# Threshold attention and a feed-forward block on one core: weight chunks begun at other points of slots six to nine, and the first loads in another order

## The chip, the core and the metric

The kernel runs on one core of a Trainium2 chip. A core has five engines that run at the same time and wait for one another by semaphores: TensorE (PE, matrix products; its weight loads are listed as PEld), VectorE (DVE), ScalarE (ACT), GpSimd (POOL) and SyncE (SP), which in this kernel only issues transfers. Each engine executes its own instructions in the order in which the program gives them. The metric is the device time of one execution in microseconds (us).

## The reference

Attention over 8 batches, 8 heads, 576 positions and head size 64, in which a score counts only if it lies within tau of the largest of its row; then a feed-forward block with a layer norm and a residual.

```python
scores = scale * np.matmul(q, k.transpose(0, 1, 3, 2))
thresh = np.max(scores, axis=-1, keepdims=True) - tau
scores = np.where(scores >= thresh, scores, -1000000000.0)
scores = scores - np.max(scores, axis=-1, keepdims=True)
attn = np.exp(scores)
attn = attn / (np.sum(attn, axis=-1, keepdims=True) + 1e-09)
x = np.matmul(attn, v)            # then (B,H,S,D) -> (B, S, H*D), 512 features
xn = (x - mean(x)) / np.sqrt(var(x) + 1e-06) * g_ln
out = x + np.maximum(xn @ w_ch1, 0.0) @ w_ch2    # 512 -> 2048 -> 512
```

q, k, v and out are 32-bit floats. The two weight matrices arrive as 64-bit floats, and the kernel turns them into 32-bit floats on the chip while attention is already running.

## The kernel before, in words

**Slots.** The work is cut into 72 slots, nine for each batch. A unit is one batch and one pair of heads. Slots 0 to 3 of a batch take the first 256 queries of the four units, slot 4 takes the 64 queries that are left over in all four, and slots 5 to 8 take the second 256 queries. One slot is a chain: `scores` (line 400) makes the scores on PE; `exponentials` (line 423) takes the row maxima on DVE (line 431), the thresholds on POOL (line 435) and the exponentials on ACT (line 445); `weights` (line 447) compares the scores with the thresholds, multiplies and sums, all in one DVE instruction of line 452 for each of four blocks. From slot 6 on POOL divides the four blocks (line 468), DVE transposes them in 32 by 32 blocks (`turn_blocks`, line 542), SP sends the result to device memory and fetches it back in another layout (lines 549 to 574), and PE multiplies with v in the following slot (`values_of`, line 611). In slots 0 to 5 PE transposes instead, by products with diagonal matrices.

**Loading.** `load_qk` fetches q and k of a unit in eight transfers, `load_v` fetches v in four (three from batch 1 on). `turn` (line 352) scales q on POOL (line 364) and transposes k and q on DVE (lines 368 to 381); `turn(u)` stands in the slot before the one that needs unit u. The q and k tiles of the units have one buffer each, so that a unit can only be loaded when the unit before it has been transposed. The first unit alone lies in the room of the tile xc, which is needed only later (`qk_room`, line 152).

**Feed-forward.** A group is half a batch, 288 tokens, and there are 16. The first layer of a group is 64 products of PE (line 801 to 806), the second layer of the first group another 64 (`second_plain`, line 835). Four parts of a slot, called quarters, each issue a share of these products (`second_part`, line 1016), so that the first group is spread over the 18 quarters from the start of slot 6. The order of PE's products is thus written out in advance; `ended` (line 321) only keeps a product from being written into the order ahead of the conversion of its weights. Two PSUM banks take the results of the products in turn, and ACT empties them (lines 809 and 848).

**Conversion of the weights.** Class `Weights` (line 178) handles 32 chunks of 128 by 512 numbers: 0 to 15 are w_ch1, 16 to 31 are w_ch2. A chunk is fetched raw (512 KB, `fetch`) into room that is free at that time, each with a note up to which chunk it may stay there. Then it takes four steps: `begin` is two DVE instructions (lines 274 and 278) that build the 32-bit number from the high word, and it queues two ACT passes over the raw words (lines 284 and 287); `carry` is an integer add on POOL (line 299) that needs both; `mask` is a DVE instruction (line 305) that needs the carry and frees the raw room; `scale` (POOL, line 315) multiplies w_ch1 by g_ln. The table `BEGUN` says for each slot up to which chunk is begun at three points: behind the row maxima and `turn`, ahead of `weights` (first number); behind `weights`, beside POOL's divisions (second); and at the end of the slot, behind the transposes of `turn_blocks` (third). `mask_all` stands ahead of the first two points and, from slot 6 on, behind `turn_blocks` (line 1164).

**Order of a slot on each engine**, as the loop from line 1085 writes it: scores; maxima; first quarter of products; `turn`; masks and begins; second quarter; carries and scales; `weights` with its divisions; masks and begins; third quarter; carries; block transposes and transfers; masks; product with v of the slot before; fourth quarter; begins; carries.

Of the kernel before, what the change touches and what calls it, by code (L numbers as in the profile page):

```python
# [12 lines left out]
ALU = mybir.AluOpType  # L13
# [5 lines left out]
def kernel(  # L19
# [31 lines left out]
    nc = tc.nc  # L51
# [4 lines left out]
    HP = H // 2  # L56
# [3 lines left out]
    NB = S // 32  # L60
# [18 lines left out]
    scl_sb = consts.tile([128, 1], F32, name="scl_sb")  # L79
# [13 lines left out]
    units = [(b, hp) for b in range(B) for hp in range(HP)]  # L93
    loaded, values_in, turned = {}, {}, {}
# [32 lines left out]
    def load_v(u):  # L127
        b, hp = units[u]
        vt = ins.tile([128, 2, J, D], F32, tag="v", name="v_in")
        vr = v_rest[hp]  # L130
        both = v[b, 2 * hp : 2 * hp + 2]
        if b:
            nc.sync.dma_start(
                out=vt.rearrange("p h c d -> p h (c d)"),
                in_=both[:, : J * 128].rearrange("h (p c) d -> p h (c d)", c=J),
            )
        for h in range(0 if b else 2):
            nc.sync.dma_start(
                out=vt[:, h], in_=both[h, : J * 128].rearrange("(c p) d -> p c d", p=128)
            )  # L140
        for j in range(2):
            nc.sync.dma_start(
                out=vr[64 * j : 64 * j + 64, j], in_=both[:, J * 128 :].rearrange("h p d -> p h d")
            )
        values_in[u] = (vt, vr)
# [8 lines left out]
    load_qk(1, (nc.sync, nc.scalar))  # L154
    for t in v_rest:
        nc.gpsimd.memset(t, 0.0)
    load_v(0)
    nc.scalar.preload_act_table_set("natural_log_exp_and_others")
    make_identity(nc, ident)
    nc.vector.memset(eps_sb, 1e-6)  # L160
# [17 lines left out]
    class Weights:  # L178
# [88 lines left out]

        def begin(self):
            i = self.begun
            assert all(self.raw[j][0] > i or self.raw[j][0] == 10 for j in range(self.masked, i))  # L270
            self.begun += 1
            hi = self.words(i, U32)[:, :, 1]
            au = self.chunks[i][0].bitcast(U32)
            nc.vector.tensor_scalar(
                out=au, in0=hi, scalar1=3, scalar2=0x3FFFFFFF,
                op0=ALU.logical_shift_left, op1=ALU.bitwise_and,
            )
            nc.vector.scalar_tensor_tensor(  # L278
                out=au, in0=hi, scalar=0xC0000000, in1=au,
                op0=ALU.bitwise_and, op1=ALU.bitwise_or,  # L280
            )
            low, low_in, top = self.words(i, I32), self.words(i, U32), self.words(i, F32)[:, :, 1]
            self.on_scalar += [
                lambda: nc.scalar.activation(
                    low[:, :, 0], low_in[:, :, 0], func=AF.Copy, scale=2.0**-29
                ),
                lambda: nc.scalar.activation(top, top, func=AF.Square),
            ]
# [59 lines left out]
    def by_blocks(n):  # L348

        return n >= FIRST  # L350

    def turn(u):

        q_in, k_in = loaded.pop(u)
        qT = att.tile([128, 2, QH], F32, tag="qT", bufs=4, name="qT")  # L360
        kT = att.tile([128, S], F32, tag="kT", bufs=4, name="kT")
        ql = q_last[u % HP]
        for at in (slice(0, 8), slice(8, NB)) if u == 0 else (slice(0, NB),):
            nc.gpsimd.tensor_scalar(
                out=q_in[:, at], in0=q_in[:, at], scalar1=scl_sb, scalar2=1.0,
                op0=ALU.mult, op1=ALU.mult,
            )
        nc.vector.transpose(kT, k_in.rearrange("p n c -> p (n c)"))
        for s in range(2):
            part = q_in[:, 9 * s : 9 * s + 8]  # L370
            if by_blocks(units[u][0] * SLOTS + units[u][1] + (HP + 1 if s else 0)):
                nc.vector.transpose(
                    qT[:, s].rearrange("p (j a c) -> p a j c", j=2, a=4),
                    part.rearrange("p (a j) c -> p a j c", j=2),
                )
            else:
                nc.vector.transpose(qT[:, s], part.rearrange("p n c -> p (n c)"))
        nc.vector.transpose(
            ql.rearrange("p (t c) -> p t c", t=2),
            q_in.rearrange("p (t n) c -> p t n c", t=2)[:, :, 8],  # L380
        )
        turned[u] = (qT, kT, ql)
# [672 lines left out]

    conversion = Weights()
    if w_ch1.dtype == I64:
        conversion.fetch(3)
    else:
        for i in range(NK):  # L1060
            nc.sync.dma_start(out=w1_sb[i], in_=w_ch1[i * 128 : (i + 1) * 128])
            nc.scalar.mul(w1_sb[i], w1_sb[i], g_sb[:, i : i + 1])
        for i in range(ND):
            nc.sync.dma_start(
                out=w2_sb[:, :, i],
                in_=w_ch2[i * 128 : (i + 1) * 128, :].rearrange("p (m c) -> p m c", m=NK),
            )
        conversion.begun = conversion.carried = len(conversion.chunks)
        conversion.masked = conversion.fetched = conversion.begun
        conversion.scaled = conversion.n1  # L1070

    BEGUN = [
        (0, 0, 2), (3, 3, 4), (5, 5, 6), (7, 7, 8), (9, 9, 10), (11, 11, 12),
        (14, 17, 19), (21, 22, 24), (26, 27, 28), (30, 31, 32), (32, 32, 32),
    ]

    def constants(times):
# [4 lines left out]

    constants(14)
    turn(0)
    for n in range(NS):
        b, s = divmod(n, SLOTS)
        masks_at, behind_at, end_at = BEGUN[min(n, len(BEGUN) - 1)]
        run(n, -3)
        if 0 < n <= HP:
            constants(8 if n > 1 else 26)  # L1090
        scores(b, s)
        run(n, -2)
        run(n, -1)
        if n == FIRST + 1:
            conversion.take(e_room[1])
        rest = exponentials(n)
        es, thr = next(rest)
        run(n, 0)
        if n == HP + 2:
            next(rest, None)  # L1100
        if n >= HP:
            conversion.fetch(3)
        run_first(stores)
        second_part(n, 0)
        while drops and drops[0][0] is nc.gpsimd:
            drops.pop(0)[-1]()
        next(rest, None)

        u = (n + 1) // SLOTS * HP + (n + 1) % SLOTS
        if (n + 1) % SLOTS < HP and u < len(units):  # L1110
            turn(u)
            if u + 1 < len(units):
                load_qk(u + 1)
        if n < HP:
            conversion.fetch(2)
        if n < SLOTS + HP:
            run_all(aside)
        conversion.mask_all()
        conversion.begin_to(masks_at)
        if n <= HP + 1:  # L1120
            conversion.carry_all()
            conversion.scale_all()
        run(n, 1)
        second_part(n, 1)
        conversion.carry_all()
        conversion.scale_all()
        blocks_go = by_blocks(n)
        diags = weights(es, thr, blocks_go)
        run_all(aside)
        drip()  # L1130
        if n < SLOTS:
            run_all(stores)
        conversion.mask_all()
        conversion.begin_to(behind_at)
        run(n, 2)
        second_part(n, 2)
        conversion.carry_all()
        box = []
        if blocks_go:
            conversion.fetch(3, wait=0)  # L1140
            scr = turn_blocks(b, s, es)
            at_quarter(n + 1, 0, lambda b=b, s=s, scr=scr, box=box: box.append(fetch(b, s, scr)))
        else:

            made = turn_weights(s, es, diags)
            for i, at in enumerate(
                (-1, -1, 0, 0)
            ):
                if i < 3:
                    at_quarter(n + 1, at, next, made)  # L1150
                else:
                    at_quarter(n + 1, at, lambda made=made, box=box: box.append(next(made)))
        at_quarter(
            n + 1, 1 if b == 0 and s <= HP else 3,
            lambda b=b, s=s, box=box: values_of(b, s, box[0]),
        )
        if s in (HP, 2 * HP):
            group_ready(2 * b + (s > HP))
        run_all(aside)
        drip({nc.vector: 4, nc.gpsimd: 6})  # L1160
        if HP <= n < FIRST:
            conversion.fetch(3)
        if n >= HP + 2:
            conversion.mask_all()
        run(n, 3)
        if b == 0 and s < HP - 1:
            load_v(s + 1)
        elif n >= SLOTS - 2 and (n + 2) % SLOTS < HP and n < NS - 2:
            load_v((n + 2) // SLOTS * HP + (n + 2) % SLOTS)
        second_part(n, 3)  # L1170
        conversion.begin_to(end_at)
        conversion.carry_all()
        run_all(aside)
        drip({nc.vector: 2, nc.gpsimd: 0})
# [40 lines left out]
```

## Time and profile before

| what | value |
|---|---|
| time, median of 3 runs | 1355.61 us (1354.12 to 1357.16) |
| time of the profiled execution | 1354.76 us |
| span of its trace | 1352.6 us |
| PE busy | 1317.1 us (97%) |
| DVE busy | 883.2 us (65%) |
| POOL busy | 630.1 us (47%) |
| ACT busy | 459.1 us (34%) |
| start of the scores of slots 6, 7, 8, 9, 10, 11 | 74.96, 100.95, 126.03, 147.40, 168.79, 187.97 us |

The profile is a page and a trace of one execution. The page has the busy time of each engine, forty slices of the span with the busy share of each in tenths, the chain of work that ended last, and groups of instructions with the mean time of one. The trace can be asked for one stretch: what each engine did in order of time, who waited for whom, and how busy each engine was. A wait is put down to whatever came last by the records. The start of a slot is read from PE's instructions of line 417. The profiled execution took 2.2 us more than its span.

### The profile page before, as it was taken

How to read it: one execution, taken by the hardware profiler on the slowest of the kernel's cores; microseconds unless marked ns; L12 is line 12 of the kernel's file. 1: busy time of each engine (PE TensorE's matmuls, PEld its weight loads, DVE VectorE, ACT ScalarE, POOL GpSimd, SP SyncE). 2: the span in 40 equal slices, each digit the busy share in tenths (PEclk: the TensorE clock that was granted, in tenths of full speed). 3: DMA queues.
4: the chain of work that ended last, by engine and by line, in shares of the span. 5: the costliest groups of instructions: out<-in, count | busy, mean ns of one | idle time of the engine just before them, and what ended most of it. 6: DMA issues, size and time to landing. Idle time of an engine off the chain costs nothing.

```text
span 1352.6 us, 40467 instructions
## 1 busy us (share of the span) xinstructions
PE 1317.1 (97%) x17400; PEld 993.9 (73%) x17400; DVE 883.2 (65%) x1544; ACT 459.1 (34%) x995; POOL 630.1 (47%) x836
## 2 busy tenths in 40 slices
PE   8997999999999999999999999999999999999997
PEld 6764557869687786968778696876869677686957
DVE  6989987667755675666766667556756667666112
ACT  4875432332423323232333323233232323323120
POOL 3567665445444444444534554444444445335313
PEclk9998999999999999999999999999999999999999
DMA  9816874457644775437744576446764376343211
GB/s 171 257 60 186 218 207 150 177 159 183 189 139 146 194 193 172 151 131 190 194 146 155 138 203 179 151 146 186 191 178 151 120 194 187 124 159 129 85 18 20
DMA packets 335300, 213.94 MB, mean 158 GB/s; under 512 B 247377, under 2 KB 292689, under 8 KB 327057
## 3 DMA queue, kind: packets, MB, share of 16 engines
q1 hardware_dynamic: 329008, 210.46, 54.2%
q8 instruction: 137, 2.24, 0.7%
q10 hardware_dynamic: 5952, 0.74, 0.4%
q0 software_dynamic: 160, 0.15, 0.1%
q14 instruction: 43, 0.34, 0.1%
HBM read 124.00 MB, written 87.29 MB: 156 GB/s over the span
## 4 chain that ended last, share of the span: by engine, by line
PE 88%; DVE 5%; DMA 2%; ACT 2%; SPq 2%; issue 1%; POOL 1%; POOLq 0%; ACTq 0%; DVEq 0%
PE p L101 36%; PE seg L101 30%; PE sc L417 10%; PE sc L611 8%; PE sc L621 2%; DVE e L452 1%; DVE w L278 1%; SPq L118 1%; PE tp L101 1%; DVE w L305 1%; ACT e L445 1%; DMA k_in<-in_k_dram 1%; DVE et L542 1%; PE var L101 1%; DVE neg L431 0%
## 5 line engine op out<-in xcount | busy, mean ns | idle before, releaser
L101 PE MATMUL p<-xc,w 128*64 128x288 f32 x4096 | 519.0, 409 | 12.1 <-ACT hidden L809 6.5
L101 PEld LDWEIGHTS p<-xc,w 128*64 128x64 f32 x4096 | 288.8, 137 | 220.0 <-issue 16.2
L431 DVE TENSOR_REDUCE neg<-sc 128x2 f32<-128x1152 f32 x144 | 188.7, 1352 | 278.1 <-PE sc L417 278.1
L468 POOL TENSOR_SCALAR e<-e,den 128x576 f32<-128x576 f32 x264 | 207.8, 799 | 135.9 <-DVE den L457 135.9
L101 PE MATMUL seg<-hidden,w 128*64 128x144 f32 x3840 | 247.9, 287 | 0.0
L101 PEld LDWEIGHTS seg<-hidden,w 128*64 128x64 f32 x3840 | 234.9, 137 | 11.5 <-issue 8.5
L452 DVE SCALAR_TENSOR_TENSOR e<-sc,thr,e 128x576 f32<-128x576 f32 x288 | 222.4, 811 | 17.9 <-POOL thr L435 11.2
L435 POOL TENSOR_SCALAR thr<-neg,low_sb 128x2 f32<-128x2 f32 x144 | 41.6, 289 | 378.0 <-DVE neg L431 377.4
L809 ACT ACTIVATE hidden<-p 128x288 f32<-128x288 f32 x256 | 106.1, 416 | 296.4 <-PE p L101 296.4
L445 ACT ACTIVATE e<-sc,neg 128x576 f32<-128x576 f32 x288 | 197.4, 753 | 2.5 <-DVE neg L431 2.5
L542 DVE STREAM_TRANSPOSE et<-e 128x1152 f32<-128x1152 f32 x118 | 161.2, 1373 | 14.3 <-POOL e L468 13.8
L417 PE MATMUL sc<-kT,qT 64*64 64x384 f32 (+3 forms) x2048 | 139.4, 403 | 3.5 <-DVE e L452 3.1
L611 PE MATMUL sc<-em,v_in 128*64 128x128 f32 (+1 forms) x2368 | 129.9, 263 | 2.9 <-DVE w L305 2.3
L611 PEld LDWEIGHTS sc<-em,v_in 128*64 128x64 f32 x2368 | 122.8, 137 | 11.5 <-DVE o L723 2.5
L101 PE MATMUL seg<-hidden,stage 128*64 128x144 f32 x1920 | 123.3, 286 | 0.0
L101 PEld LDWEIGHTS seg<-hidden,stage 128*64 128x64 f32 x1920 | 117.6, 137 | 2.9 <-issue 2.9
L634 ACT COPY x<-sc 128x128 f32<-128x128 f32 x120 | 31.6, 265 | 236.2 <-PE sc L417 171.0
L882 POOL TENSOR_TENSOR hidden<-hidden 128x576 f32<-128x576 f32 x60 | 84.8, 1428 | 51.9 <-ACT hidden L809 42.3
L417 PEld LDWEIGHTS sc<-kT,qT 64*64 64x64 f32 x2048 | 76.1, 133 | 44.5 <-issue 20.9
L897 ACT COPY part<-seg 128x288 f32<-128x288 f32 x74 | 29.8, 403 | 190.6 <-PE seg L101 190.1
L882 DVE TENSOR_TENSOR hidden<-hidden 128x576 f32<-128x576 f32 x60 | 51.2, 888 | 51.5 <-PE seg L101 48.5
L818 POOL TENSOR_TENSOR hidden<-hidden 128x288 f32<-128x288 f32 x48 | 38.9, 810 | 54.6 <-ACT hidden L816 52.1
(131 smaller groups left out, 1093.7 us busy)
## 6 DMA issues: line engine op xcount, KB each, us to landing
scr<-et SPq DMA_DIRECT2D x63, 1152.0 KB, 5.0
em<-scr SPq DMA_DIRECT2D x63, 1024.0 KB, 5.8
q_in<-in_q_dram SPq DMA_DIRECT2D x124, 72.0 KB, 2.7
out_dram<-ot SPq DMA_DIRECT2D x248, 36.0 KB, 3.8
k_in<-in_k_dram SPq DMA_DIRECT2D x120, 72.0 KB, 3.0
er<-scr SPq DMA_DIRECT2D x132, 64.0 KB, 5.2
v_in<-in_v_dram SPq DMA_DIRECT2D x28, 256.0 KB, 5.5
w<-in_moe_w_ch_dram SPq DMA_DIRECT2D x11, 512.0 KB, 6.4
```

Source lines behind the costliest of these rows:

```text
L101: nc.tensor.matmul(out[r], lhsT=lhsT[:, r], rhs=rhs, **flags)
L417: nc.tensor.matmul(sc[h][64 * i : 64 * i + 64, at : at + n], lhsT=ql[r] if s == HP else qT[r, half, j * 128 + 64 * i : j * 128 + 64 * i + 64],
L431: nc.vector.tensor_reduce(out=neg[:, i], in_=pairs[h], axis=AXL.X, op=ALU.max, negate=True,)
L435: nc.gpsimd.tensor_scalar(out=thr[:, i], in0=neg[:, i], scalar1=-1.0, scalar2=low_sb, op0=ALU.mult, op1=ALU.add,)
L445: nc.scalar.activation(es[:, i], blocks[i], func=AF.Exp, bias=neg[:, i : i + 1])
L452: nc.vector.scalar_tensor_tensor(out=es[:, i], in0=blocks[i], scalar=thr[:, i : i + 1], in1=es[:, i], op0=ALU.is_ge, op1=ALU.mult, accum_o ...
L468: nc.gpsimd.tensor_scalar(out=es[:, i], in0=es[:, i], scalar1=den[:, i : i + 1], scalar2=1.0, op0=ALU.mult, op1=ALU.mult,)
L542: nc.vector.transpose(et[:, :, 64 * h : 64 * h + 64].rearrange("p n (j c) -> p j n c", j=2), es[:, 2 * h : 2 * h + 2].rearrange("p j (n c) ...
L611: nc.tensor.matmul(dst[64 * h : 64 * h + 64], lhsT=vt[:, h, c, :], rhs=pick(em[:, 2 * j : 2 * j + 2, c], h), start=c == 0 and first, stop= ...
L809: nc.scalar.activation(hidden[:, d], p1, func=AF.Relu)
L818: nc.gpsimd.tensor_tensor(out=sq[:, 0], in0=sq[:, 0], in1=sq[:, c], op=ALU.add)
L882: eng.tensor_tensor(out=out[at], in0=in0[at], in1=in1[at], op=op)
```

## The change

Three things are altered.

The loads at the start. The first two raw chunks are fetched ahead of everything but the first two units. The third unit's q and k go into the first unit's room (`qk_room`), as soon as that unit has been transposed; v of the first unit and two more chunks follow. The fourth unit is loaded where the third was, one slot earlier than it was before, and the fifth again where it was.

Scaling q. For units 1 to 3 POOL's scaling is taken out of `turn` and stands ahead of the row maxima of the slot (`scale_q`).

The conversion. In slots 6 to 9 the table has two or three chunks at the first point, three (in slot 9 two) at the second and none at the end of a slot. The masks behind `turn_blocks` are gone, so that chunks begun at the second point are masked in the next slot, behind its maxima. The check in `begin` on how long a raw chunk may lie in the room of a later one is widened by six chunks.

```diff
-    load_v(0)
     nc.scalar.preload_act_table_set("natural_log_exp_and_others")
...
-            assert all(self.raw[j][0] > i or self.raw[j][0] == 10 for j in range(self.masked, i))
+            assert all(self.raw[j][0] + 6 > i or self.raw[j][0] == 10 for j in range(self.masked, i))
...
+    def scale_q(u, q_in):
+
         for at in (slice(0, 8), slice(8, NB)) if u == 0 else (slice(0, NB),):
             nc.gpsimd.tensor_scalar(
                 out=q_in[:, at], in0=q_in[:, at], scalar1=scl_sb, scalar2=1.0,
                 op0=ALU.mult, op1=ALU.mult,
             )
+
+    def turn(u):
...
+        if not 0 < u < HP:
+            scale_q(u, q_in)
...
     if w_ch1.dtype == I64:
-        conversion.fetch(3)
+        conversion.fetch(2)
...
         (0, 0, 2), (3, 3, 4), (5, 5, 6), (7, 7, 8), (9, 9, 10), (11, 11, 12),
-        (14, 17, 19), (21, 22, 24), (26, 27, 28), (30, 31, 32), (32, 32, 32),
+        (15, 18, 18), (20, 23, 23), (25, 28, 28), (30, 32, 32),
...
     turn(0)
+    load_qk(2, room=qk_room.rearrange("p c t -> p (c t)"))
+    load_v(0)
+    conversion.fetch(2)
     for n in range(NS):
...
+        if n + 1 < HP:
+            scale_q(n + 1, loaded[n + 1][0])
         rest = exponentials(n)
...
             turn(u)
-            if u + 1 < len(units):
-                load_qk(u + 1)
+            if u + 1 < len(units) and u != 2:
+                load_qk(u + 1 if u > 1 else 3)
         if n < HP:
-            conversion.fetch(2)
+            conversion.fetch(2 if n else 1)
...
         if HP <= n < FIRST:
             conversion.fetch(3)
-        if n >= HP + 2:
-            conversion.mask_all()
         run(n, 3)
```

More of the change, by code (lines that the diff above doesn't have):

```diff
@@ L350, in by_blocks @@
         return n >= FIRST
[L352 to L362, printed above, removed]
+    def scale_q(u, q_in):
         for at in (slice(0, 8), slice(8, NB)) if u == 0 else (slice(0, NB),):
@@ L367, in turn @@
             )
+    def turn(u):
+        q_in, k_in = loaded.pop(u)
+        if not 0 < u < HP:
+            scale_q(u, q_in)
+        qT = att.tile([128, 2, QH], F32, tag="qT", bufs=4, name="qT")
+        kT = att.tile([128, S], F32, tag="kT", bufs=4, name="kT")
+        ql = q_last[u % HP]
         nc.vector.transpose(kT, k_in.rearrange("p n c -> p (n c)"))
```

## The prediction

> **What bounds the kernel now.** I read the page first. PE is busy 97% of the span, so most of the run can only be moved by PE's idle time. The busy slices show where that lies: the first ninth.
>
> ```profile
> PE 1317.1 (97%) x17400; PEld 993.9 (73%) x17400; DVE 883.2 (65%) x1544; ACT 459.1 (34%) x995; POOL 630.1 (47%) x836
> ...
> DVE  6989987667755675666766667556756667666112
> ```
>
> Then engine time per stretch, one stretch from scores to scores for each of slots 6 to 10 (columns: us, and busy time of PE, PEld, DVE, ACT, POOL).
>
> ```profile
> 74.96:100.95 25.99, 25.04 (x273) 16.44 (x277) 20.28 (x34) 17.32 (x34) 17.72 (x23) 1.00 0.01 2
> 100.95:126.03 25.08, 18.54 (x181) 10.81 (x176) 24.77 (x35) 12.07 (x25) 19.33 (x18) 0.86 0.71 199
> 126.03:147.40 21.37, 18.72 (x196) 11.21 (x192) 20.68 (x34) 10.67 (x21) 12.13 (x14) 1.00 0.77 172
> 147.40:168.79 21.39, 18.73 (x196) 11.48 (x192) 20.73 (x35) 9.18 (x18) 14.32 (x15) 1.00 0.89 233
> 168.79:187.97 19.18, 17.54 (x189) 10.59 (x184) 16.62 (x32) 6.31 (x13) 11.12 (x15) 1.00 0.78 202
> ```
>
> In slots 7 to 9 DVE is the full engine (24.77 of 25.08), PE idles 2.6 to 6.5 us a slot. In slot 6 DVE has a gap. From slot 11 on PE is full, so what slots 0 to 10 win or lose is passed on unchanged to the end. The waits, of DVE (8 to 200 us) and of PE (80 to 190 us), name the gaps (us in total, times, longest):
>
> ```profile
> DVE w L305 <- POOL w L299: 5.3, 1, 5.3
> ...
> DVE kT L368 <- DMA k_in<-in_k_dram: 1.8, 1, 1.8
> DVE qT L377 <- POOL q_in L364: 0.9, 2, 0.4
> ```
>
> ```profile
> PE p L101 <- ACT hidden L809: 9.0, 2, 6.5
> PE sc L611 <- DVE w L305: 2.3, 1, 2.3
> PE p L101 <- DVE w L305: 1.6, 1, 1.6
> ```
>
> The 1.8 and 0.9 us are the opening: slots 1, and 0 and 2. The 5.3 us are slot 6, first mask against first carry. PE's 1.6 us are at 178.04, in slot 10: the products of the last chunk (31) wait for its mask (177.33, line 305). That wait ends the stage.
>
> The timeline (start, duration) gives the price of a begin, here two in slot 8:
>
> ```profile
> 137.09 0.42 DVE L274 TENSOR_SCALAR w<-e 128x512 uint32<-128x512 uint32 x1
> 137.54 0.69 DVE L278 SCALAR_TENSOR_TENSOR w<-e,w 128x512 uint32<-128x512 uint32 x1
> 138.15 0.42 DVE L274 TENSOR_SCALAR w<-x_room 128x512 uint32<-128x512 uint32 x1
> 138.61 1.72 DVE L278 SCALAR_TENSOR_TENSOR w<-x_room,w 128x512 uint32<-128x512 uint32 x1
> ```
>
> The first takes 137.09 to 138.15, 1.06 us. The second takes 2.10, because POOL began the first one's carry at 138.47 (1.31 us). Beside divisions (slot 6, 97.01 to 99.83, two begins) one takes 1.41. A mask alone takes 0.60.
>
> [...] 0.69 us becomes 1.72, about the rest of the carry. [...] SP stood at the transfer of line 549 for 34.4 us from slot 5 to 6.
>
> **The change, part by part.** All sums are against the profiled execution, 1354.76 us (span 1352.6 plus 2.2 around it), 0.85 under the median; I add the same difference to the median, 1355.61.
>
> *Opening.* Unit 2's eight transfers were issued at 15.24 to 22.36, behind 1.5 MB of chunks (issued 11.34 to 13.92), and k landed at 24.6, when DVE had been free since 22.95. Now SP issues two chunks (about 8.4 to 9.4, behind unit 1's q, which ended at 8.35), unit 2 (its room is free at 9.15; eight at 0.5 to 0.6 us: to about 15), four of v, two chunks, unit 3, one chunk. Estimated from those rows, k of unit 2 lands near 19, before it is needed at 22.5: the 1.79 us go. So do the 0.45 us in slot 0: POOL scales q ahead of the thresholds, under PE's scores and the maxima; in slot 0 the scaling waits for unit 1's q (8.35 plus some 4 us of landing, 12.3), and the thresholds queued behind it on POOL are wanted by `weights` only at 14.65. In slot 2 the 0.44 us also go from DVE, but PE's warm-up products run from 40.76 right up to the scores at 42.60, so there PE becomes last and nothing is won. Chunk 2, begun at about 25.2, is issued near 17.5 and lands some 5.5 us later (the median at that time): covered by 2 us. v of unit 0 is wanted at 24.8 and lands near 21. Sum: -2.2. Two-sided bound: -2.7 if PE gives way, +1 if a chunk in front delays unit 1's k (needed at 13.06).
>
> *Slots 6 to 9 on DVE.* All 21 begins (12 to 32) and masks remain; only their neighbours change. I walk each slot with the prices above, up to the maxima of the next.
> Slot 6: one begin more ahead of the masked scores falls into the 5.3 us wait, free. The first carry still ends at 92.8 (POOL's sums of squares at 88.95 to 91.52 hold it). Three masks follow carries at 1.27 us each: to about 97.1. Three begins beside divisions (4.2): 101.3. Transposes (2.55): 103.9, against 108.92 before, where three masks (3.45) and two begins (3.1) followed. -5.0.
> Slot 7: one mask more beside scales (+0.8). After `weights` come the root of the variance (2.7) and two masks, by which time the divisions are done; of the three begins the second and third meet the carries of the one before: 2 x 2.1 = +4.2. Gone: a mask and two begins behind the transposes (0.57 + 1.06 + 2.06). +1.3.
> Slot 8: one mask more (+0.6). Only two of four divisions outlast `weights` (143.76 to 146.30), and two masks and one begin use them up (143.59 to 146.76): again two begins beside carries, +4.2. Gone: mask and begin at 149.65 to 151.91, -2.3. They had covered POOL's residual add at 149.80; now the output transpose waits for it, +1.0. +3.5.
> Slot 9: two masks more (+1.2), begin 31 beside a carry (+2.1), gone mask and begin 170.21 to 171.84 (-1.6). +1.7.
> Sum: -5.0 + 1.3 + 3.5 + 1.7 = +1.5 at slot 10's maxima. The title's "beside divisions only" holds in slot 6 alone. Two-sided bound on the five begins beside carries (7, 8, 9): 5 x 1.04 = 5.2 us less if ACT's passes (line 284), and so the carries, come too late to meet them; 2 us more if the first begins of the rows collide too.
>
> *What PE waits for then.* Mask 30 was behind slot 9's transposes; now it stands where mask 31 stood. Eight products of PE need chunk 30 or 31, not four, and the mean of group 1 lies between. After the wait PE has 8 x 0.485 + 0.48 = 4.36 us to the first product of group 1, against 4 x 0.485 = 1.94. +2.4. DVE's scaling of x (line 686) and slot 10's transposes come later behind it; the product that uses them was at 200.99 and em's fetch at 191.59, some 5 us of cover.
> Waits earlier on PE (chunk 15's scale in slot 7, mask 25 in slot 9) grow by 1 to 3 us each, but PE reaches the scores some 3 us before DVE: nothing.
>
> *SP.* Chunk 31 is now fetched in slot 9 behind em and er of slot 8, not in slot 8. er ended at 161.5 before; the issue comes near 163, and with 6.4 us (the median landing) the chunk is there at 169.4. DVE wants it at 168.5; that wait lies beside the carry which would have held it anyway: nothing.
>
> Sum: -2.2 + 1.5 + 2.4 = +1.7: 1356.5 in the profiled execution, **1357.3** against the median.
>
> **Rivals.**
> *Faster: the carries miss the begins.* At 92.8 POOL was late because ACT was held by PE's results; were that so in slots 7 to 9, five begins cost 1.06. 1357.3 - 5.2 = 1352.1. Against it: in slot 8 the carry followed each begin within 0.25 us.
> *Begins do lie beside divisions*, as the title says: 5 x 0.69 less, 1353.9.
> *Slower: the opening's wait moves on.* Place: unit 1's k (ACT's queue) or chunk 2, with 1 MB of chunks now ahead. Nothing is won once DVE gets k of unit 2 or chunk 2 1.8 to 2.2 us late, that is k after 24.7 or chunk 2 after 27.4. 1357.3 + 2.2 = 1359.5. For it: DMA is 90% busy from 9 us on. Against: big packets moved 340 to 416 GB/s at 15 to 18 us.
> *Slower: chunk 31.* Slow landings of 9.4 us (slot 5's) would put it at 172.4, 2.3 us behind the cover of the carry at 170.1; with masks 25 to 27 late too, about 1360.5. It decides above a landing of 7 us.
>
> **How the numbers follow.** About 0.2% (2.7 us) is what a measurement of this kernel can tell from no change: faster is below 1352.9, slower above 1358.3. Chances: main sum 0.45 (own range 1355 to 1360; 0.27 same, 0.18 slower); carries miss 0.17 (0.14 faster, 0.03 same); begins beside divisions 0.06 (0.05 same, 0.01 faster); opening lost 0.20 (0.04 same, 0.16 slower); chunk 31 0.12 (0.02 same, 0.10 slower). Together faster 0.15, same 0.41, slower 0.44. Range: 1352.2, the faster rival, to 1361, past the slower ones.
>
> **What the profile after would show.** Opening right: no wait of DVE on k_in, scores of slot 3 (42.60) at about 40.4. Slot 7's maxima near 101.7 (108.92 less 5.0 and 2.2). Line 278 at over 1.6 us seven or eight times in slots 6 to 9, not four (107.3, 129.8, 138.6, 158.9). PE waiting for line 305 in slot 10 four products earlier, for several us. I am wrong if slot 10's mask 30 comes earlier than mask 31 did less 2.2 us (175.1), or if SP's queue holds chunk 31.

## The result, and the profile after

The changed kernel takes 1358.84 us (median of 9 runs, 1357.59 to 1360.26), the kernel before, run alongside, 1354.66 (9 runs, 1353.91 to 1357.16): a ratio of 1.0029, interval 1.0019 to 1.0039. It is 4.2 us slower; I had forecast 1.7 us slower. The profiled execution took 1360.19 us with a span of 1358.1, 5.5 us more than that of before. It is one of the slowest of the nine, 1.35 us above their median, so the two profiles lie further apart than the medians do. One execution of the variants below, of pe_kept_busy, ran at a mean granted clock of 0.56 from end to end (2300 us) and counts in no ratio.

In the changed kernel the mask is line 304, the carry 298, a begin 273 and 277, the maxima 435 and the scores 421; L101 is the helper that records most products. The page, busy time and DVE's slices:

```profile
PE 1320.2 (97%) x17400; PEld 993.8 (73%) x17400; DVE 885.2 (65%) x1544; ACT 459.3 (34%) x995; POOL 630.0 (46%) x836
...
DVE  7989967766755675666766667556756667666112
```

No engine has more instructions to run. DVE is busy 2.0 us longer and PE, with the same 17400 matmuls, 3.1 us longer. That last number is the odd one: equal work should take equal time. The stretches from scores to scores of slots 6 to 10 show where (us, then busy time of PE, PEld, DVE, ACT, POOL; then PE's granted clock):

```profile
73.94:101.22 27.28, 25.48 (x272) 16.25 (x276) 22.59 (x37) 17.89 (x34) 19.00 (x24) 1.00 0.01 2
101.22:119.65 18.43, 16.85 (x181) 10.13 (x177) 17.95 (x29) 9.39 (x22) 15.64 (x15) 1.00 0.78 210
119.65:147.49 27.84, 20.84 (x197) 12.63 (x192) 27.08 (x38) 13.99 (x26) 16.31 (x16) 0.94 0.74 179
147.49:167.80 20.31, 18.50 (x196) 11.52 (x192) 18.74 (x34) 7.59 (x14) 11.51 (x14) 1.00 0.89 232
167.80:193.14 25.34, 20.12 (x188) 11.61 (x184) 18.69 (x32) 6.67 (x14) 12.30 (x16) 0.87 0.69 181
```

Up to slot 10's scores nothing is lost (167.80 against 168.79). Slot 10 then takes 25.34 us where it took 19.18, and slot 11's scores stand at 193.14 against 187.97: +5.17, and the distance stays between 5.2 and 5.8 to the end. In this row PE is busy 20.12 us with 188 matmuls; before it was 17.54 with 189. Its clock column reads 0.87.

The waits of DVE (8 to 200 us), then of PE (80 to 195 us):

```profile
DVE neg L435 <- PE sc L421: 6.0, 3, 4.6
DVE w L304 <- POOL w L298: 4.3, 1, 4.3
DVE xc L690 <- PE mean L101: 3.6, 1, 3.6
...
DVE w L273 <- DMA hidden<-in_moe_w_ch_dram: 1.4, 1, 1.4
```

```profile
PE p L101 <- DVE w L304: 5.2, 1, 5.2
...
PE p L101 <- ACT hidden L813: 5.0, 5, 2.5
```

Three things are new. PE waits 5.2 us for a mask, where it waited 1.6. DVE in turn waits 3.6 us for the mean from PE, and 4.6 us for scores in slot 11, both behind that one wait. And the opening's wait for k of unit 2 is gone, but one of 1.4 us for chunk 2 has come. Group 1 is the second group of tokens; its first products are the ones from xc. The timeline of PE in slot 10 (start, duration; four matmuls of the records are one product):

```profile
169.85 3.13 PE L101 MATMUL p<-hidden,w 128*64 128x288 f32 x24
178.21 3.15 PE L101 MATMUL p<-hidden,w 128*64 128x288 f32 x12 [5.22 <-DVE w L304]
181.14 1.17 PE L101 MATMUL mean<-sum,avg_sb 128*64 128x288 f32 x4
182.10 3.27 PE L101 MATMUL p<-hidden,w 128*64 128x288 f32 x20
185.21 4.53 PE L101 MATMUL p<-xc,w 128*64 128x288 f32 x36
```

The same place in the kernel before:

```profile
178.04 2.16 PE L101 MATMUL p<-hidden,w 128*64 128x288 f32 x16 [1.65 <-DVE w L305]
180.03 4.54 PE L101 MATMUL p<-xc,w 128*64 128x288 f32 x36
```

Ahead of the wait 24 matmuls take 3.13 us, behind it 12 of the same take 3.15. From the end of the wait to the first product of group 1 it is 7.00 us (1.99 before), not the 4.36 that I had counted. The changed kernel's stretch in windows, columns as above:

```profile
172.98:178.20 5.22, 0.01 (x1) 0.00 (x0) 4.77 (x9) 2.80 (x5) 2.59 (x5) 0.85 0.89 265
178.20:179.80 1.60, 1.59 (x8) 0.86 (x10) 0.56 (x1) 0.00 (x0) 0.00 (x0) 0.50 0.70 221
...
183.00:185.20 2.20, 2.20 (x18) 1.22 (x16) 2.20 (x6) 0.00 (x0) 0.00 (x0) 0.89 0.65 105
```

The granted clock falls to a half during the wait, some 3.7 us into it, and comes back only near 183.4, after 5.2 us of products: half of those, 2.6 us, are lost. The kernel before has the same, in a place where it cost nothing: slot 7's wait of 6.5 us, windows of PE around it:

```profile
105.65:112.19 6.54, 0.01 (x1) 0.01 (x1) 6.47 (x8) 3.94 (x9) 4.41 (x6) 0.79 0.88 222
112.19:116.20 4.01, 4.01 (x18) 2.07 (x20) 3.94 (x7) 2.48 (x5) 3.18 (x3) 0.50 1.01 259
```

18 matmuls in 4.01 us; DVE, busy for 3.94 of them, hid it. The number that told of it, 0.86 in the clock column of slot 7, stands in the view that the prediction shows first.

The products behind the waits of 5.22 and 6.54 us ran at a granted clock of 0.50. Behind slot 10's wait of 1.65 us in the kernel before it was 1.00 (178.04 to 182), and behind one of 2.62 us it was 0.52 (old_begins_two_masks, below); the last section puts the waits side by side.

So the new theory, the **clock theory**: slot 10's loss is the wait for mask 30, the 4 products and the mean that it now holds up (+2.4, as forecast), and 2.6 us of half clock, which the wait itself brings about.

### The profile page after: what moved, and what is told of

It is laid out like the page before. It is cut to its first block, busy times and chain, and to the rows that moved or that the text cites. A ratio compares the mean times of both kernels' runs of the same rounds, so it can differ in the third digit from the quotient of the medians.

```text
span 1358.1 us, 40472 instructions
## 1 busy us (share of the span) xinstructions
PE 1320.2 (97%) x17400; PEld 993.8 (73%) x17400; DVE 885.2 (65%) x1544; ACT 459.3 (34%) x995; POOL 630.0 (46%) x836
## 4 chain that ended last, share of the span: by engine, by line
PE 87%; DVE 3%; DMA 3%; SPq 3%; ACT 2%; issue 1%; POOL 0%; POOLq 0%; DVEq 0%; ACTq 0%
PE p L101 34%; PE seg L101 30%; PE sc L421 10%; PE sc L615 8%; PE sc L625 2%; DVE e L456 1%; ACT e L449 1%; DMA em<-scr 1%; PE tp L101 1%; SPq L118 1%; DMA k_in<-in_k_dram 1%; DVE et L546 1%; PE mean L101 1%; SPq L553 1%; PE var L101 0%
## 5 line engine op out<-in xcount | busy, mean ns | idle before, releaser
L101 PE MATMUL p<-xc,w 128*64 128x288 f32 x4096 | 517.8, 408 | 7.7 <-ACT part L901 4.6
L101 PEld LDWEIGHTS p<-xc,w 128*64 128x64 f32 x4096 | 286.9, 137 | 216.4 <-issue 14.3
L101 PE MATMUL seg<-hidden,w 128*64 128x144 f32 x3840 | 247.9, 287 | 0.0
L101 PEld LDWEIGHTS seg<-hidden,w 128*64 128x64 f32 x3840 | 234.9, 137 | 11.5 <-issue 8.5
L101 PE MATMUL seg<-hidden,stage 128*64 128x144 f32 x1920 | 123.3, 286 | 0.0
L101 PEld LDWEIGHTS seg<-hidden,stage 128*64 128x64 f32 x1920 | 117.6, 137 | 2.9 <-issue 2.9
```

The lines of the kernel that those rows point to most:

```text
L101: nc.tensor.matmul(out[r], lhsT=lhsT[:, r], rhs=rhs, **flags)
```

## Experiments

All are variants of the changed kernel except where said. Times are medians; ratios are to the kernel before, run alongside (medians 1354.62 to 1354.92 us). A ratio is not the quotient of the two medians and differs from it by up to 0.0007, 1 us; where two variants were not run side by side, their intervals say more than the difference of their medians.

**PE kept busy.** Constants go through PE where it would idle, with no use made of the products:

```diff
         conversion.begin_to(masks_at)
+        if n == SLOTS + 1:
+            constants(20)
```

> The changed kernel, with 20 products of constants (into a free bank, results unused) put on PE between the 24 products before mask 30 of slot 10 and those that wait for it. At 0.23 us each (as in the opening) they fill 4.6 of the 5.2 us of idling and end before the mask (178.16). Clock theory: of the 5.2 us lost, 2.64 are the products after the wait at half the granted clock (7.00 us from mask 30 to the first product of group 1, against 4.36 counted); PE kept busy keeps the clock at 1.00, and the time falls by 2.6, from 1358.8 to 1356.2. Rival, the place theory: the products are slow there for another reason (transfers of 300 to 400 GB/s at 178 to 183 us, operands just written), and the time stays at 1358.8 with the 7.0 us unchanged.

> The same kernel as pe_kept_busy (20 products of constants ahead of the wait for mask 30), for its profile, since the profiled execution of the first was at about half the clock from end to end. Clock theory: PE's clock column reads 1.00 from 173 to 185 us, and from mask 30's end to the first product of group 1 it takes about 4.4 us (7.05 in the changed kernel). If half clock is only part of it, more than 5 us at clock 1.00.

Measured: 1356.97 us, ratio 1.0013 (1.0007 to 1.0020), so 1.9 us below the changed kernel's median (the two intervals just touch), where 2.6 had been expected; the single run of the second gave 1356.26. PE's timeline in the second:

```profile
171.65 4.54 PE L101 MATMUL warm<-ident,avg_sb 128*64 128x128 f32 x80
...
177.52 1.68 PE L101 MATMUL p<-hidden,w 128*64 128x288 f32 x12 [0.86 <-DVE w L304]
...
181.94 4.54 PE L101 MATMUL p<-xc,w 128*64 128x288 f32 x36
```

From the wait's end to group 1 it is now 4.42 us, with the clock at 1.00 in every window from 172.9 to 186; 12 matmuls take 1.68. DVE's part and the mask's place are as in the changed kernel. The transfers are there too (283 and 304 GB/s at 177.6 to 182), so the place theory falls: 4.42 is the 4.36 that I had worked out, and the other 2.6 us are the clock, in these two profiles. The medians show 1.9 of the 2.6; why not all is not shown. Adding work to PE made the kernel faster.

**The parts alone.** First the opening alone, from the changed kernel. The third call of the masks is the call of `mask_all` behind `turn_blocks`, which the change had taken out:

```diff
-        (15, 18, 18), (20, 23, 23), (25, 28, 28), (30, 32, 32),
+        (14, 17, 19), (21, 22, 24), (26, 27, 28), (30, 31, 32), (32, 32, 32),
...
             conversion.fetch(3)
+        if n >= HP + 2:
+            conversion.mask_all()
         run(n, 3)
```

> The changed kernel with the old table of begins and the third call of the masks back: only the opening's part of the change is left. Opening theory: it gains 1.0 us (as slot 3's scores, 42.61 to 41.61, show in the changed kernel), not the 2.2 that I forecast, since chunk 2 lands late: 1353.7 against 1354.7, slot 10's mask 31 at about 176.3. Rival: the forecast's 2.2 would have come without the new begins, then 1352.5. Second rival: slot 6 or SP's queue takes the 1.0 back, then 1354.7.

Measured: 1354.00 us, ratio 0.9989 (0.9980 to 0.9997): 0.8 us won, near the first value (the interval, -2.7 to -0.4 us, holds the rival's 2.2 as well). Its profiled execution is no guide to the opening, since half clock fell on slot 2's scores there (28 matmuls in 3.85 us, 2.16 elsewhere; granted clock 0.55 from 31.2 to 35).

Then the conversion alone: the kernel before, with the new table, without the third call of the masks, and with the wider assertion.

```diff
-        (14, 17, 19), (21, 22, 24), (26, 27, 28), (30, 31, 32), (32, 32, 32),
+        (15, 18, 18), (20, 23, 23), (25, 28, 28), (30, 32, 32),
...
-        if n >= HP + 2:
-            conversion.mask_all()
```

> The kernel before with the new table of begins, the third call of the masks gone, and the wider assertion: only the conversion's part of the change. Clock theory: DVE's mask 30 comes 1.2 us later than mask 31 did (+1.2), 4 products more and the mean after it (+2.4), half clock after the idling (+2.6): +6.2, 1360.9. If the two parts are not additive, because the later opening lets PE's idling stay short of what brings the clock down, +3.6: 1358.3.

Measured: 1359.32 us, ratio 1.0040 (1.0028 to 1.0053): 4.5 us lost, between the two values. The parts add up: -0.8 + 4.5 = +3.7, against +4.2 for both. In its profile PE idles only 3.49 us for mask 30 and the clock falls all the same, just after PE has resumed (1.00 in the wait, 0.63 in the first 0.80 us behind it, then 0.50); from there to group 1 it is 6.11 us, 1.7 more than at full clock.

**Chunk 2 first**, the other term that was off. In the changed kernel SP's timeline reads:

```profile
10.01 4.30 SPq L118 DMA_DIRECT2D qk_room<-in_q_dram  x4
14.36 4.09 SPq L118 DMA_DIRECT2D qk_room<-in_k_dram  x4
...
22.45 1.07 SPq L257 DMA_DIRECT2D hidden<-in_moe_w_ch_dram  x2
```

Unit 2's eight transfers hold SP for 8.4 us, and chunk 2 is issued at 22.45 and landed 3.9 us later, 1.4 us after DVE wanted it.

```diff
-        conversion.fetch(2)
+        conversion.fetch(3)
...
     load_v(0)
-    conversion.fetch(2)
+    conversion.fetch(1)
```

> The changed kernel with chunk 2 fetched together with chunks 0 and 1, ahead of unit 2's q and k (one chunk in place of two behind v). Opening theory: DVE's wait for chunk 2 (1.4 us) goes; k of unit 2 comes about 1 us later, near 20, still before 22.1; PE's warm-up then ends last in slots 2 and 3 (28.65 against scores at 29.07), so 0.4 to 1.0 us is won: 1358.8 becomes 1357.8 to 1358.4. If nothing but DVE bound the opening, the whole 1.4: 1357.4.

Measured: 1358.80 us, ratio 1.0029 (1.0019 to 1.0038): nothing, a miss. The wait for chunk 2 is gone, DVE does not wait for k, and slot 3's scores come at 40.35, where the prediction had put them (40.4; the changed kernel 41.60). Slot 10's scores are 1.6 us earlier (166.21) and slot 11's 1.2 (191.90), PE's wait for mask 30 being 5.56 us. The profiled execution is 1.3 us shorter than the changed kernel's, but that one lay 1.35 above its own median and this one lies on it: the pair of profiles overstates the gain, and what the medians lose again is not shown. With the masks mended (below) the same edit gives medians lower by 0.8 and 1.45 us, but the intervals of the ratios overlap almost wholly, so a gain of this edit is not shown there either.

**Mask 30 ahead of the maxima.** The third call of the masks in slot 9 alone:

```diff
+        if n == SLOTS:
+            conversion.mask_all()
         run(n, 3)
```

> The changed kernel with the third call of the masks back in slot 9 alone, so that masks 30 and 31 stand behind slot 9's transposes, ahead of slot 10's maxima (about 172 to 173.3). Clock theory with the place of mask 30 as the whole cause: PE does not idle there, the clock stays at 1.00, the first product of group 1 then waits for DVE's scaling of x at about 179.2 instead of 185.2: 6 us less than the changed kernel, 1352.8 to 1353.9. Rival: the begins in slots 7 to 9 are what costs, and the masks' place only shows it: then the wait moves on to the next thing that DVE delivers, and less than 3 us come back, 1356 or more.

Measured: 1354.20 us, ratio 0.9991 (0.9983 to 0.9999), 4.6 us below the changed kernel. PE's timeline in slot 10:

```profile
171.09 4.59 PE L101 MATMUL p<-hidden,w 128*64 128x288 f32 x36
...
179.88 4.59 PE L101 MATMUL p<-xc,w 128*64 128x288 f32 x36 [0.55 <-ACT o L852]
```

Masks 30 and 31 stand at 172.1 and 172.7, PE waits for neither, and group 1 starts at 179.88 instead of 185.21. The place of mask 30 is the cause of the loss. The time is 0.3 to 1.4 us more than expected. Ahead of group 1 PE waits 0.52 us for POOL's sum and 0.55 for ACT, and the clock falls once more, in slot 9 after two short waits (0.78 and 1.62 us):

```profile
160.60:163.50 2.90, 0.51 (x8) 0.28 (x6) 2.83 (x10) 0.59 (x2) 2.37 (x4) 1.00 1.01 274
163.50:167.60 4.10, 4.10 (x37) 3.38 (x39) 4.03 (x7) 0.90 (x2) 4.10 (x4) 0.60 0.79 155
```

That fall is not what kept the rest back: both_mended (below) keeps the clock at 1.00 there, and from DVE's first instruction of `weights` in slot 9 to group 1 it takes 20.12 us as against 20.11 here. What did is open.

**Table or masks.** The remaining two of the four combinations. In the first only the old table is put back, in the second only the third call of the masks, from slot 6 on.

> The changed kernel with the old table of begins, and the third call of the masks still gone: it tells the table from the masks. Masks theory (what costs is that mask 30 comes behind slot 10's maxima, whichever table): masks 30 and 31 both stand there, mask 30 at about 175.7 to 176.4, PE idles some 3.4 us for it and has 4.4 us to go to group 1 (7 if the clock falls): 0.7 to 3.3 us behind the kernel before, 1355.3 to 1357.9. Table theory (what costs is the begins' place): like opening_alone, 1354.0.

> The changed kernel with the third call of the masks back in every slot from slot 6 on, and the new table of begins. Masks theory: only the one in slot 9 counts, so it is like third_mask_slot9: 1353.7 to 1354.7. Table theory: the new begins still cost DVE 1.4 us in slots 6 to 9, and it stands that much behind opening_alone: 1355.4.

| median, us (ratio's interval) | third call gone | third call from slot 6 on | in slot 9 alone |
|---|---|---|---|
| old table | 1355.66 (0.9999 to 1.0015) | 1354.00 (0.9980 to 0.9997) | - |
| new table | 1358.84 (1.0019 to 1.0039) | 1355.96 (0.9999 to 1.0015) | 1354.20 (0.9983 to 0.9999) |

Without the third call the old table loses too, 1.7 us against the same table with it: mask 30 comes behind the maxima, at 175.16, PE idles 2.62 us, the clock falls right after (0.52 from 175.86 to 179.40), and it takes 6.1 us to group 1. That is the masks theory's value. The new table with all three calls is a miss for it: 1355.96, not 1353.7 to 1354.7, and nearer to the table theory's 1355.4. In that profile three masks stand between the transposes and the next maxima in slots 6 and 7: slot 7's maxima come at 105.76 (103.38 in the changed kernel), slot 8's at 129.55 (126.16), slot 10's at 175.05 (172.59). So the third call is needed in slot 9 whichever the table; that with the new table it is in the way in slots 6 and 7 is what this one profile suggests.

**Towards a faster kernel.** Chunk 2 first, with each of the two good places for the masks:

> The changed kernel with chunk 2 first and the third call of the masks back in slot 9 alone. The two add up: third_mask_slot9 (1354.2) less 0.4 to 1.0: 1353.2 to 1353.8, faster than the kernel before (1354.8). If in slots 9 and 10 DVE and PE, which end within 0.6 us of each other there, pass the gain on unchanged, 1353.2; if slot 8's half clock, which comes and goes, takes it, 1354.2.

> The opening alone (old begins, three calls of the masks) with chunk 2 first: opening_alone (1354.0) less 0.4 to 1.0: 1353.0 to 1353.6. Against both_mended it tells what the new table of begins is worth by itself: if the new begins' +1.2 on DVE counts, this one is the faster of the two by up to 1.2; if PE bounds slots 9 and 10 with the masks back, the two are the same within 0.5.

Measured: 1353.37 (0.9984 to 0.9997) with the new table and slot 9's masks, 1352.55 (0.9979 to 0.9992) with the old table and all three. The two were run alongside; the old table is the better one by 0.8 us in the medians, though the intervals overlap. So the new row was kept only where the changed kernel gains on DVE, in slot 6:

```diff
-        (15, 18, 18), (20, 23, 23), (25, 28, 28), (30, 32, 32),
+        (15, 18, 18), (21, 22, 24), (26, 27, 28), (30, 31, 32), (32, 32, 32),
...
+        if n > HP + 2:
+            conversion.mask_all()
         run(n, 3)
```

> A try at the best of both: chunk 2 first, the new row of begins in slot 6 alone with no third masks there, the old rows and three calls of the masks from slot 7 on. Slot 6 is where the changed kernel gains on DVE (4.5 us to slot 7's maxima), slots 8 and 9 where it loses (3.4 and 2.2). DVE theory: one mask and one begin more in slot 7 (2 to 2.7 us), the rest as before: DVE reaches slot 10 some 2 us before old_begins_chunk2_first, up to where PE bounds: 1350.6 to 1352. PE theory: in slots 9 and 10 PE is what bounds the kernel once it doesn't wait for masks 30 and 31, and nothing is won on old_begins_chunk2_first: 1352.5.

> The same with the third call of the masks in slot 9 alone. Against slot6_new_rest_old it tells what the third call in slots 7 and 8 does: masks that wait there for a carry in front of the maxima (as in new_begins_three_masks) would make this one the faster by 1 us or so; if the masks there only change places, the two are the same within 0.5 us.

Measured: 1350.86 (0.9955 to 0.9980) and 1351.21 (0.9965 to 0.9985), the same for both within their intervals: 4.1 and 3.7 us faster than the kernel before. PE in slot 10 of the first:

```profile
174.35 2.16 PE L101 MATMUL p<-hidden,w 128*64 128x288 f32 x16 [1.65 <-DVE w L304]
176.34 4.54 PE L101 MATMUL p<-xc,w 128*64 128x288 f32 x36
```

It is the shape of before (16 matmuls behind a wait of 1.65 us at full clock), 3.7 us earlier. The PE theory falls: DVE's gain in slot 6 does reach the end, if slots 7 to 9 don't spend it. Two things differ in slot 6, the row and the missing third call; which of them counts is not told apart.

## Why the prediction was right or wrong

The direction was right, and so was most of the mechanism; the size was 2.5 us short (4.2 for 1.7). That 1357.3 came within 1.5 us of 1358.84 is in part luck: it was counted from 1355.61, the median of three runs, and nine gave 1354.66. The upper end of the forecast was argued from the opening and from chunk 31; the half clock stands in none of the rivals. By its own steps, in the profiled executions:

| step | forecast | measured |
|---|---|---|
| opening | -2.2 | -1.0 (slot 3's scores 42.60 to 41.60) |
| slots 6 to 9 on DVE | +1.5 | +1.2 (mask 30 ends at 178.16, mask 31 ended at 177.99, with the opening's 1.0 off) |
| products and mean behind the mask | +2.4 | +5.0 (7.00 us against 1.99) |
| sum, at slot 11's scores | +1.7 | +5.2 |

*Opening: mechanism right, size off, by my own misreading.* I took unit 2's eight transfers at 0.5 to 0.6 us each. They took 1.05 each, and the kernel before already had 0.63 for q and 1.14 for k:

```profile
15.24 2.53 SPq L118 DMA_DIRECT2D q_in<-in_q_dram  x4
17.81 4.55 SPq L118 DMA_DIRECT2D k_in<-in_k_dram  x4
```

So chunk 2 was issued at 22.45, not 17.5. The rival "the opening's wait moves on" named chunk 2 as a place, and half of it came true: chunk 2 landed at 26.4, inside the 27.4 from which all would have been lost. The pair of profiles is not the last word on it: conversion_alone, with the old opening, waited only 0.9 us for k and had slot 3's scores at 41.66. The medians give 0.8 us for the opening.

*Slots 6 to 9: right in the sum, and slot by slot within 1 us.* From maxima to maxima: slot 6 -4.5 (forecast -5.0; PE's scores end last there by 0.2), slot 7 +0.3 (+1.3), slot 8 +3.4 (+3.5), slot 9 +2.2 (+1.7). (The title that the prediction quotes, "beside divisions only", is not the one above; the words are about the second number of the table.) In slot 6 the working has a slip: 92.8 and three masks at 1.27 are 96.6, not 97.1, so it should have read -5.5. The second and third of the begins meet carries, here in slot 8:

```profile
142.57 1.67 DVE L277 SCALAR_TENSOR_TENSOR w<-y_room,w 128x512 uint32<-128x512 uint32 x1
...
144.62 1.67 DVE L277 SCALAR_TENSOR_TENSOR w<-stage,w 128x512 uint32<-128x512 uint32 x1
```

The carries began at 142.34 and 144.38 and took 1.36 us each; with no carry beside it, the first begin of slot 8's earlier pair had 0.69 on line 277 (132.91). Line 277 is over 1.6 us seven times, as forecast, and each of the seven starts less than 0.4 us behind the start of a carry, so both rivals, that the begins miss the carries and that they lie beside divisions, are out.

*Behind the mask: the step that failed.* "8 x 0.485 + 0.48 = 4.36" holds at full clock (4.42 with PE kept busy), and at the clock that was granted it took 7.00. The term prices the products as if the wait in front of them left PE's clock unchanged. The prediction's own times gave the wait: 24 products end near 173, mask 30 near 177.3, some 4.3 us. A gap of 6.5 us with half clock behind it lay in the same trace. With 2.6 us more, 1.2 less won by the opening and 0.3 less on DVE, 1356.5 for the profiled execution becomes 1360.0; it took 1360.19.

*Chunk 31.* SP issued it at 160.41 and it landed 5.5 us later, ahead of its begin: no wait, and that rival is out, though the issue came earlier than I had put it (163). *SP's queue and PE's waits in slots 7 to 9*: they cost nothing, as forecast; PE's half clock in slot 8 (0.94 in the windows) was covered by DVE.

## What to carry to other kernels

A wait of PE had two prices here: slot 10's cost its length, 5.22 us, and 2.6 us more for the products behind it at half clock. Read the granted clock beside every gap, and where a gap can't be closed, try products of constants in it: in slot 10 they were worth 1.9 us in the medians. Count what is queued behind a late event, not only how late it is: DVE came 1.2 us later to the mask, and the place of the masks in slot 9 cost 4.6 us. Where a change gains in one stage and loses in others, keep the stage: the new row in slot 6 alone, without the third call there, is worth 1.7 us over the old table in the medians, though the intervals of the two just touch.

## What the runs showed of the hardware

- PE's granted clock fell to 0.50 behind some of its waits and stayed at 1.00 behind others. In the profiled executions, windows of PE:

| run, slot | wait of PE, us | granted clock in the wait | behind it |
|---|---|---|---|
| before, 7 | 6.54 | 0.79 | 0.50 for 4.01 us |
| changed kernel, 10 | 5.22 | 0.85 | 0.50 from 178.20 to 183.00 |
| conversion_alone, 10 | 3.49 | 1.00 | 0.63 for 0.80 us, then 0.50 |
| old_begins_two_masks, 10 | 2.62 | 1.00 | 0.52 for 3.54 us |
| third_mask_slot9, 8 | 2.50 | 1.00 | 1.00 for 0.80 us, then 0.63 and 0.50 |
| changed kernel, 8 | 2.50 | 1.00 | 1.00 for 8.00 us |
| before, 8 | 2.45 | 1.00 | 1.00 for 8.00 us |
| before, 10 | 1.65 | 1.00 | 1.00 for 3.96 us |

- The half clock lasted 6.83 us in slot 7 of the kernel before (109.40 to 116.23), and 3.41 us in slot 8 (142.51 to 145.92) and 6.83 us in slot 10 (176.64 to 183.47) of the changed one. Of the last 6.83 us, 5.26 fell on products.
- The length of one wait does not tell the two cases apart: of the waits of 2.50 us in slot 8, one kept the clock and one lost it. Nor do two waits together. third_mask_slot9, shown above, and both_mended have the same two waits in slot 9 (0.78 and 1.62 us; 0.77 and 1.62). both_mended has them 0.42 us earlier. third_mask_slot9 loses the clock 0.9 us after PE has resumed; both_mended keeps it, at 1.00 in every window from 161.45 to 171.04:

```profile
161.45:163.04 1.59, 0.00 (x0) 0.01 (x1) 1.55 (x7) 0.00 (x0) 1.40 (x3) 1.00 0.89 220
163.04:163.84 0.80, 0.78 (x14) 0.80 (x16) 0.80 (x3) 0.00 (x0) 0.80 (x1) 1.00 1.16 311
163.84:164.64 0.80, 0.80 (x19) 0.80 (x17) 0.80 (x1) 0.00 (x0) 0.80 (x2) 1.00 1.12 194
164.64:165.44 0.80, 0.80 (x12) 0.59 (x10) 0.77 (x3) 0.00 (x0) 0.80 (x1) 1.00 0.95 156
```

- What decides between them is not shown.
